# Attention with decay, then an expert layer: the first unit's second product taken by halves of the output columns, its weights loaded by the same halves, and a third score bank in the first four slots

## The chip, the core and the metric

The kernel runs on one core of a Trainium2 chip. Five engines work side by side on it, each through its own list of instructions in order: TensorE (PE in the profile; PEld is its loading of weights), VectorE (DVE), ScalarE (ACT), GpSimd (POOL) and SyncE (SP). They wait for each other through semaphores. DMA transfers are issued by POOL (through a software queue), SP and ACT. PSUM, where TensorE writes, has eight banks of 512 fp32 columns per partition.

The metric is the device time of one execution in microseconds, the median of several runs. Before the change it is 342.13 us (three runs, 341.74 to 342.63).

## The reference

Eight batches of eight heads, 576 positions, 64 elements a head. Scores get a decay that comes from cumulated logarithms of `f`, a causal mask and a softmax; the heads' outputs, side by side, are 4608 tokens of 512. The expert layer follows.

```python
scores = scale * np.matmul(q, k.transpose(0, 1, 3, 2))
log_f = np.log(np.clip(f, 0.0001, 1.0))
cum = np.cumsum(log_f, axis=-1)
scores = np.where(causal, -1e9, scores + (cum[:, :, :, None] - cum[:, :, None, :]))
attn = softmax(scores)
x = concat_heads(np.matmul(attn, v))          # 4608 x 512
h = x @ w_in                                  # 512 x 2048
out = (h - np.tanh(h)) @ w_out                # 2048 x 512
```

## The kernel before

The order of all instructions is written out by hand (`manual_schedule` over all five engines): what Python calls first stands first in its engine's list.

**Slots.** The work of attention goes by pairs of heads, 32 pairs (8 batches of 4). Pair p is computed in slot p, and `att_items(p)` lists what a slot holds: seven score tiles (ti = 0 to 6) of pair p, the transposes of q and k for pair p + 1, the second attention product of pair p - 1 (`values`), and the turning of that product into the ring `XR` that feeds the expert layer (`turn`). `LOADS` hangs DMA loads and some vector work on places (slot, ti).

- `scores` (L357 to L376): a tile of scores goes to a PSUM bank, ScalarE takes the exponential (L366) into a tile `e`, and from batch 1 on POOL cuts it causally (L376). In batch 0 (slots 0 to 3) a small matmul with `late` (L360) does the cut. The banks come from the pool `ps_sc` (two buffers); in batch 0 the small tile ti = 3 has the bank of `ps_tr`.
- `trans` (L303, copies L314 on ScalarE, L316 on VectorE): six transposes of q or k into one bank, then two copies (even and odd positions) into `QT` or `KT`. `copies` says which engine makes which copy: "VV" both VectorE.
- `values` (L394): 15 small matmuls a head; then `divide` on VectorE (L403 to L405) makes `xn`.
- `turn`: in batch 0 five transposes on TensorE (L422) and a copy on ScalarE (L423) into `XR`; later two transposing DMAs.
- `unread(n)` (L567): n matmuls of 128 columns whose result nobody reads. `start` issues 99 of them; in slot 0 `att_items` adds 4 at ti = 0, 5 and 6 each, and in slots 1 to 3 it adds 2 at ti = 0 and 2 at ti = 6.

**The expert layer** goes by units of 512 tokens. `mlp1` (L453) makes 16 tiles of the first product; ScalarE takes tanh (L458) and VectorE adds (L464) into `GQ`. For unit 0 `mlp2_plain` (L494) makes the second product: 16 steps of four matmuls with 512 columns; four steps fill a bank with 128 tokens by 512 output columns over all 16 tiles of `GQ`, four tiles a step, and ScalarE copies the bank out (L498). The later units use seven products of half size instead of eight (`mlp2`, L518), with sums of weights that `weights` makes once on VectorE (L283) at the places `SPOTS`. Steps of this layer are spread over the slots from slot 4 on (`TAKE`).

**Loads.** POOL issues nearly all loads in order into one software queue with eight semaphores, so the n-th load waits until the one eight before it has landed. `bulk` issues what is left of batch 0 (q, then k for heads 4 to 7, the decay rows chi, cq and clo, then v). The weights `w_in` come in two halves in slots 1 and 2, `w_out` in two halves of its rows in slot 4, and behind them q and k of batch 2.

Of the kernel before, what the change touches and what calls it, by code (L numbers as in the profile page):

```python
# [21 lines left out]
def kernel(  # L22
# [191 lines left out]

    def bulk():
        (k_hi, chi_0), (k_lo, clo_0), (q_hi, cq_0) = aug_rows(0)
        load_qk(qn, q, 0, 4, H)
        nc.gpsimd.dma_start(out=k_hi, in_=chi_0)
        load_qk(kn, k, 0, 4, H)
        nc.gpsimd.dma_start(out=q_hi, in_=cq_0)  # L220
        nc.gpsimd.dma_start(out=k_lo, in_=clo_0)
        for n in range(NJ - 1):
            load_v_block(0, n, 2, H)

# [1 line left out]
        nc.gpsimd.dma_start(out=win[:, :, f0:f1],  # L226
                            in_=moe_w_in[:, f0:f1].rearrange("(c p) f -> p c f", p=P))

    def load_wout(t0, t1):
        nc.gpsimd.dma_start(out=wout[:, t0:t1, :],  # L230
                            in_=moe_w_out[t0 * P:t1 * P, :].rearrange("(t p) e -> p t e", p=P))

    LOADS = {(0, 1): [lambda: load_qk(qn, q, 1, 0, 2), lambda: load_qk(kn, k, 1, 0, 2)],
             (0, 4): [lambda: load_qk(qn, q, 1, 2, 4), lambda: load_qk(kn, k, 1, 2, 4)],
# [2 lines left out]
             (1, 5): [lambda: load_qk(kn, k, 1, 4, H)],  # L237
             (2, 1): [lambda: load_v_rest(1), lambda: load_v_head(1, 0)],
             (2, 4): [lambda: load_v_head(1, 1), lambda: load_win(DFF // 2, DFF)],
             (4, 0): [lambda: load_wout(0, NFT // 2)],  # L240
             (4, 2): [lambda: load_wout(NFT // 2, NFT)]}
    for n in range(NJ - 1):
        LOADS.setdefault((3, n), []).append(lambda n=n: load_v_block(1, n, 2, H))
    def add(where, fn, *args):
        LOADS.setdefault(where, []).append(lambda: fn(*args))

    for b in range(2, B):
        p0 = (b - 1) * NPAIR
        at_q = [(p0 - 2, n + 2) for n in range(NJ)]
        at_k = [(p0, n) for n in range(NJ)]  # L250
        at_v = [(p0 + 1, n) for n in range(NJ)]
        to_q, to_k = (p0 - 1, 1), (p0 + 1, 4)
        on_q = p0
        on_k = (p0 + 3, 0), (p0 + 3, 2), (p0 + 4, 1), (p0 + 4, 4)
        if b == FAR:
            at_q = [(p0 - 1, n) for n in range(NJ)]
            to_q, on_q = (p0, 4), p0 + 3
            on_k = (p0 + 3, 2), (p0 + 3, 4), (p0 + 4, 0), (p0 + 4, 4)
        add((p0, 0), load_aug, b)
        for n in range(NJ):  # L260
            if n < NJ - 1:
                add(at_v[n], load_v_block, b, n, 0, H)
            else:
                add(at_v[n], load_v_rest, b)
            if b < FAR:
                continue
            add(at_q[n], load_block, qb, q, b, n)
            add(at_k[n], load_block, kb, k, b, n)
            add(to_q, turn_block, TQ[b % 2], qb, b, n)
            add(to_k, turn_block, TK, kb, b, n)  # L270
        if b < FAR:
            add((p0, 5), load_qk, qn, q, b, 0, H)
            add((p0, 6), load_qk, kn, k, b, 0, H)
            continue
        for n, (c, a) in enumerate(((0, 0), (0, 1), (2, 0), (2, 1))):
            add(on_k[n], place, KT, TK, b, a, c, 2, "V")
            add((on_q, (1 if b == FAR else 3) + n), place, QT, TQ[b % 2], b, a, c // 2, 1, "A")
            if c:
                add((on_q + 1, 1 + 2 * a), place, QT, TQ[b % 2], b, a, c, 2, "V")
# [2 lines left out]
        ks = slice(n * NK // 2, (n + 1) * NK // 2)  # L282
        nc.vector.tensor_tensor(out=o[:, ks, :], in0=x[:, ks, :], in1=y[:, ks, :], op=ALU.subtract)  # L283

    SPOTS = [(7, 1), (7, 3), (7, 5), (8, 1), (8, 3), (8, 5), (9, 5), (10, 5)]
    for i, (o, x, y) in enumerate(((W1, B12, B11), (W2, B22, W1), (W4, B21, W2), (B12, B22, B12))):
        for n in range(2):
            LOADS.setdefault(SPOTS[2 * i + n], []).append(lambda o=o, x=x, y=y, n=n: weights(o, x, y, n))
# [51 lines left out]
             4: (0, 1, 1, P), 5: (0, 1, 1, P), 6: (0, 2, 320, P)}  # L340

    def scores(b, c, ti):
        if b == 0 and ti == LAST:
            ps = ps_tr.tile([P, UW], FP32, tag="tr", name="ps")
        else:
            ps = ps_sc.tile([P, 512], FP32, tag="sc", name="ps")
# [62 lines left out]
        if not hold:  # L409
            release()  # L410

    def turn(b, c):
        xn = XN.pop((b, c))
        r0 = b % 4 * S
        if b == 0:
            x32 = m_bank("x32")
            if c == NPAIR - 1:
                M_AT[0] -= 1
            xt = x32.bitcast(FP16)[:, 0:S]
            for ib in (NJ - 1, 0, 1, 2, 3):  # L420
                w0 = min(ib * P, S - P)
                nc.tensor.transpose(out=xt[:, w0:w0 + P], in_=xn[:, ib, :], identity=id16)  # L422
            nc.scalar.activation(out=XR[:, c, r0:r0 + S], in_=xt, func=AF.Copy)  # L423
            return
        nc.sync.dma_start_transpose(out=XR[:, c, r0:r0 + S - D].rearrange("p (n t) -> p n t", t=P),
                                    in_=xn[:, 0:NJ - 1, :].rearrange("p n d -> p (n d)"))
        nc.sync.dma_start_transpose(out=XR[:, c, r0 + S - D:r0 + S], in_=xn[D:P, NJ - 1, :])
# [58 lines left out]
        nc.vector.tensor_tensor(out=LHS[name](u, i)[:, ks], in0=LHS[x](u, i)[:, ks], in1=LHS[y](u, i)[:, ks], op=op)  # L486

    def mlp2_plain(u, s):
        m, part = divmod(s, 4)
        if part == 0:  # L490
            M2[u] = bank("ops")
        ops = M2[u]
        for ft in range(part * 4, part * 4 + 4):
            nc.tensor.matmul(out=ops, lhsT=GQ[(u, ft % NK // 4)][:, ft // NK, ft % 4, m * P:(m + 1) * P],  # L494
                             rhs=wout[:, ft, :], start=(ft == 0), stop=(ft == NFT - 1))
        if part == 3:
            ost = tmp.tile([P, DM], FP32, tag="ost", name="ost", bufs=3)
            nc.scalar.activation(out=ost, in_=ops, func=AF.Copy)  # L498
            r0 = u * UW + m * P
            nc.sync.dma_start(out=out[r0:r0 + P, :], in_=ost)  # L500

    STEPS = [("A11", B11, "x"), ("S3", B12, "y"), ("A12", B21, "x"), ("S2", W2, "y"),
             ("S1", W1, "v"), ("A22", W4, "z"), ("S4", B22, "v")]
# [57 lines left out]
        else:  # L561
            give(0, 1, plus, M2["m7"])

    def unread(n):
        idle = ps_tr.tile([P, UW], FP32, tag="tr", name="idle")
        for i in range(n):
            nc.tensor.matmul(out=idle[:, i % 4 * P:i % 4 * P + P], lhsT=warm, rhs=warm, start=True, stop=True)  # L567

# [33 lines left out]
    def att_items(p):  # L602
        def put(fn, *args):
            items.append((lambda: fn(*args), True))
# [6 lines left out]
        for ti in range(len(TILES)):  # L611
            if here and (p > 0 or ti > 1):
                put(scores, *here, ti)
            if p == 1 and ti == 6:
                items.append((lambda: const_rows(1), False))
                items.append((lambda: load_aug(1), False))
            if early and ti in (0, 6) or p == 0 and ti == 5:
                put(unread, 2 if p else 4)
            if p == 1 and ti == 3:
                put(last)  # L620
            for load in LOADS.get((p, ti), ()):
# [10 lines left out]
                if ti in (4, 5):  # L632
                    put(mlp1, 0, ti - 4, 1)
            if ti == at_k and p < 2 * NPAIR - 1 and p != NPAIR:
                put(trans, *after, kn, KT, early, "VV")
            if p == NPAIR:
                if ti == 1:
                    put(turn, *pairs[p - 2])
                    put(values, *before)
                    put(mlp1, 0, 0, 0)  # L640
                elif ti == 2:
                    put(mlp1, 0, 1, 0)
                    put(turn, *before)
                    put(trans, *after, kn, KT, early, "VV")
            elif early and ti in (2, 3) and before:
                put(values, *before, (ti - 2,))
            elif not early and ti == 2 and before:
                put(values, *before, (0, 1), p == NPAIR + 2)
            if p < NPAIR:
                if ti == 1 and p > 1:  # L650
                    put(turn, *pairs[p - 2])
            elif p > NPAIR and ti == 3:
                items.append((release, False))
                put(turn, *before)
# [65 lines left out]
```

## Time and profile before

| | before |
|---|---|
| median of the runs | 342.13 us (341.74 to 342.63) |
| the profiled execution | 341.94 us |
| its span (first to last instruction) | 340.2 us |
| TensorE busy | 332.2 us (98%) |
| VectorE busy | 263.2 us (77%) |
| ScalarE busy | 235.0 us (69%) |
| POOL busy | 161.6 us (48%) |
| share of TensorE in the chain that ended last | 95% |
| first TensorE work of slots 1, 2, 3 and 4 | 14.74, 18.90, 23.53, 28.14 us |

The profile gives, for each engine, how long it was busy and, before an instruction, how long the engine sat idle and what ended that idle time. A row of the timeline reads: start in us, duration in us, engine, line, operation, output <- inputs with their shapes, how many are merged, and in brackets the idle time in front and its releaser. Matmuls are pipelined: a row's duration holds the latency of its last matmul, so the next row can start before it ends, and a bracket counts less than the hole between two rows of work.

### The profile page before, as it was taken

The page shows a single profiled execution, that of the slowest core. Times are in us where ns is not written, and L with a number is a line of the kernel's source. Part 1 is how long each engine was busy: PE and PEld are TensorE (multiplying, and loading weights), DVE is VectorE, ACT ScalarE, POOL GpSimd, SP SyncE. Part 2 cuts the span into 40 slices and gives each one's busy share as a digit, 9 for nine tenths or more (in the row PEclk, how much of TensorE's full clock was granted, in tenths as well). Part 3 has the DMA queues.
Part 4 walks back from the last instruction along what each step waited for, and adds up shares of the span by engine and source line. Part 5 has one row for each costly group of instructions (what it writes and reads, how often), then busy time and mean ns, then how long its engine had stood idle before and what let it go on. Part 6 is the DMA issues. An engine that isn't in the chain of part 4 may idle for free.

```text
span 340.2 us, 8658 instructions
## 1 busy us (share of the span) xinstructions
PE 332.2 (98%) x3271; PEld 231.8 (68%) x3271; DVE 263.2 (77%) x516; ACT 235.0 (69%) x440; POOL 161.6 (48%) x321
## 2 busy tenths in 40 slices
PE   8889999999999999999999999999999999999995
PEld 8676555555588458855788888656875686486485
DVE  8898888658887788678967886688668766966864
ACT  6887777888987886778677867787558742632630
POOL 8876746685657673776377547632322210000000
PEclk9999999999999999999999999999999999999999
DMA  9999999999999998999999998990131023002003
GB/s 121 146 181 200 190 200 168 170 145 161 135 100 177 157 116 90 130 186 120 115 114 168 129 125 99 178 124 13 51 113 14 19 59 102 0 33 92 3 14 109
DMA packets 144941, 38.86 MB, mean 114 GB/s; under 512 B 128188, under 2 KB 143276, under 8 KB 144900
## 3 DMA queue, kind: packets, MB, share of 16 engines
q0 software_dynamic: 92512, 18.39, 74.2%
q1 hardware_dynamic: 52356, 19.88, 30.7%
q8 instruction: 25, 0.41, 0.5%
q14 instruction: 16, 0.13, 0.1%
q10 hardware_dynamic: 32, 0.06, 0.1%
HBM read 36.90 MB, written 9.44 MB: 136 GB/s over the span
## 4 chain that ended last, share of the span: by engine, by line
PE 95%; ACT 3%; issue 1%; DVE 0%; ACTq 0%
PE hps L453 37%; PE ops L518 29%; PE ps L357 13%; PE av L394 9%; PE ops L494 3%; PE idle L567 2%; ACT e L366 2%; PE t L303 2%; PE ps L360 1%; PE x L422 0%; ACT W L575 0%; ACT KT L314 0%; ACT XR L423 0%; ACT W L314 0%; ACT th L458 0%
## 5 line engine op out<-in xcount | busy, mean ns | idle before, releaser
L453 PE MATMUL hps<-XR,win 128*128 128x512 f16 (+1 forms) x640 | 140.9, 357 | 0.3 <-ACT XR L423 0.2
L458 ACT ACTIVATE th<-hps 128x512 f32<-128x512 f32 x144 | 86.6, 602 | 55.1 <-PE hps L453 52.4
L366 ACT ACTIVATE e<-ps 128x512 f16<-128x512 f32 x192 | 110.5, 598 | 10.8 <-PE ps L357 6.9
L464 DVE TENSOR_TENSOR gq<-hps,th 128x512 f16<-128x512 f32 x144 | 98.2, 687 | 24.9 <-ACT th L458 23.4
L376 POOL TENSOR_SCALAR_AFFINE_SELECT e<-e 128x128 f16<-128x128 f16 x168 | 59.9, 358 | 71.9 <-ACT e L366 69.5
L453 PEld LDWEIGHTS <-win 128*128 128x128 f16 x640 | 57.7, 97 | 48.7 <-issue 0.7
L357 PE MATMUL ps<-QT,KT 67*128 67x512 f16 (+1 forms) x372 | 74.4, 276 | 2.2 <-ACT e L366 1.8
L518 PEld LDWEIGHTS <-gq 128*128 128x128 f16 x640 | 60.3, 97 | 11.1
L518 PE MATMUL ops<-wout,gq 128*128 128x256 f16 x512 | 63.2, 272 | 0.0
L357 PEld LDWEIGHTS <-KT 67*128 67x128 f16 x372 | 35.5, 98 | 24.3 <-issue 1.3
L394 PEld LDWEIGHTS <-e 128*128 128x128 f16 x896 | 32.3, 97 | 3.8
L394 PE MATMUL av<-vn,e 128*128 128x65 f16 x896 | 33.6, 193 | 0.0
L131 POOL DMA_DIRECT2D vn<-in_v_dram x32 | 27.9, 876 | 7.3 <-DMA win<-in_moe_w_in_dram 3.0
L518 PE MATMUL ops<-W,sq 128*128 128x256 f16 x256 | 31.2, 272 | 0.0
L405 DVE TENSOR_TENSOR xn<-av,rs 128x640 f16<-128x640 f32 x32 | 26.4, 825 | 1.1
L518 PEld LDWEIGHTS <-sq 128*128 128x128 f16 x256 | 24.2, 98 | 3.4
L376 POOL TENSOR_SCALAR_AFFINE_SELECT el<-el 128x128 f16<-128x128 f16 x28 | 9.2, 330 | 27.8 <-ACT el L366 27.3
L108 POOL DMA_DIRECT2D kn<-in_k_dram x25 | 21.1, 845 | 1.5 <-issue 1.3
L108 POOL DMA_DIRECT2D qn<-in_q_dram x25 | 21.1, 845 | 1.4 <-issue 0.9
L403 DVE TENSOR_SCALAR rs<-av 128x10 f32<-128x10 f32 x32 | 5.2, 163 | 19.0 <-PE av L394 17.8
L533 ACT ACTIVATE m<-ops 128x512 f32<-128x512 f32 x16 | 9.5, 596 | 10.9 <-PE ops L518 10.9
L486 DVE TENSOR_TENSOR gq<-gq 128x512 f16<-128x512 f16 x32 | 16.6, 519 | 0.0
(92 smaller groups left out, 317.6 us busy)
## 6 DMA issues: line engine op xcount, KB each, us to landing
out_dram<-ost SPq DMA_DIRECT2D x34, 256.0 KB
vn<-in_v_dram POOLq DMA_DIRECT2D x24, 128.0 KB, 5.6
qn<-in_q_dram POOLq DMA_DIRECT2D x20, 128.0 KB, 5.0
kn<-in_k_dram POOLq DMA_DIRECT2D x20, 128.0 KB, 4.7
win<-in_moe_w_in_dram POOLq DMA_DIRECT2D x2, 1024.0 KB, 12.2
wout<-in_moe_w_out_dram POOLq DMA_DIRECT2D x2, 1024.0 KB, 14.9
XR<-xn SPq DMA_TRANSPOSE x56
vn<-in_v_dram POOLq DMA_DIRECT2D x12, 64.0 KB, 5.3
```

Source lines behind the costliest of these rows:

```text
L108: nc.gpsimd.dma_start(out=dst[b % 2][0:pn, n, :].rearrange("p (h d) -> p h d", h=H), in_=src[b, :, n * P:n * P + pn, :].rearrange("h p d - ...
L131: nc.gpsimd.dma_start(out=vn[b % 2][:, n, h0:h1, 0:D], in_=v[b, h0:h1, n * P:(n + 1) * P, :].rearrange("h p d -> p h d"))
L357: nc.tensor.matmul(out=ps[:, col:col + n], lhsT=kt[0:rows, h, j * P:(j + 1) * P], rhs=qt[0:rows, h, i0:i0 + n], start=True, stop=cut == 0)
L366: nc.scalar.activation(out=e[:, lo:hi], in_=ps[:, lo:hi], func=AF.Exp, scale=qscale)
L376: nc.gpsimd.affine_select(out=view, in_=view, compare_op=ALU.is_ge, fill=0.0, base=0, pattern=pat, channel_multiplier=-1)
L394: nc.tensor.matmul(out=av[:, a, ib, :], lhsT=E.pop((b, c, a, j, ib)), rhs=vn[b % 2][:, j, 2 * c + a, 0:D + 1], start=(j == 0), stop=(j == ib))
L405: nc.vector.tensor_tensor(out=xn.rearrange("p i (a d) -> p a i d", a=2), in0=av[:, :, :, 0:D], in1=rs.to_broadcast([P, 2, NJ, D]), op=ALU. ...
L453: nc.tensor.matmul(out=hps[:, o:o + n], lhsT=win[:, ci, ft * P:(ft + 1) * P], rhs=XR[:, ci, t:t + n], start=(ci == 0), stop=(ci == NCH - 1))
L458: nc.scalar.activation(out=th, in_=hps, func=AF.Tanh, scale=-1.0)
L464: nc.vector.tensor_tensor(out=GQ[(u, i)][:, half, kt, :], in0=hps, in1=th, op=ALU.add)
L486: nc.vector.tensor_tensor(out=LHS[name](u, i)[:, ks], in0=LHS[x](u, i)[:, ks], in1=LHS[y](u, i)[:, ks], op=op)
L518: nc.tensor.matmul(out=ps[:, m, :], lhsT=LHS[lhs](u, kt // 4)[:, kt % 4, m * P:(m + 1) * P], rhs=rhs[:, kt, :], start=(fresh and (apart or ...
```

## The change

- **Second product of unit 0.** A step of `mlp2_plain` now makes eight matmuls with 256 columns: for one half of the output columns (e), one pair of token blocks (mp), one block of it (m) and one half of the 16 tiles of `GQ`. Four steps still fill one bank, now two blocks of 128 tokens by 256 columns. The first step reads tiles 0 to 7, the second tiles 8 to 15.
- **Loads of w_out** go by the same halves of the columns: the first at (4, 0), the second at (5, 1). q and k of batch 2 move up to (4, 2) and (4, 5), so they are issued between the two. v of batch 2 moves from slot 5 to slot 6, q of batch 3 by one tile within slot 7.
- **The sums of weights** (`SPOTS`) move from slots 7 to 10 into slots 8 to 10.
- **Loads of batch 0** (`bulk`): q and k of heads 4 and 5, then the decay rows, then q and k of heads 6 and 7.
- **Slots 0 to 3.** In slots 1 to 3 every third score tile goes to the bank of `ps_tr`, so three banks take turns; in slot 0 nothing changes there. `values` of the second head comes after ti = 4 instead of ti = 3. In slots 2 and 3 the copy into `XR` is on VectorE instead of ScalarE, and the first of the two copies of k on ScalarE instead of VectorE.
- **Unread matmuls**: slot 0 gets 2, 14, 4 and 6 at ti = 0, 2, 5 and 6; slot 1 gets 8 at ti = 6 in a bank of `ps_m`; slots 2 and 3 get none.

```diff
     def bulk():
-        load_qk(qn, q, 0, 4, H)
+        load_qk(qn, q, 0, 4, 6)
+        load_qk(kn, k, 0, 4, 6)
         nc.gpsimd.dma_start(out=k_hi, in_=chi_0)
-        load_qk(kn, k, 0, 4, H)
         nc.gpsimd.dma_start(out=q_hi, in_=cq_0)
         nc.gpsimd.dma_start(out=k_lo, in_=clo_0)
+        load_qk(qn, q, 0, 6, H)
+        load_qk(kn, k, 0, 6, H)
...
-    def load_wout(t0, t1):
-        nc.gpsimd.dma_start(out=wout[:, t0:t1, :],
-                            in_=moe_w_out[t0 * P:t1 * P, :].rearrange("(t p) e -> p t e", p=P))
+    def load_wout(e0, e1):
+        nc.gpsimd.dma_start(out=wout[:, :, e0:e1], in_=moe_w_out[:, e0:e1].rearrange("(t p) e -> p t e", p=P))
...
-             (4, 0): [lambda: load_wout(0, NFT // 2)],
-             (4, 2): [lambda: load_wout(NFT // 2, NFT)]}
+             (4, 0): [lambda: load_wout(0, HE)],
+             (5, 1): [lambda: load_wout(HE, DM)]}
...
-        at_v = [(p0 + 1, n) for n in range(NJ)]
+        at_v = [(p0 + (1 if b >= FAR else 2), n) for n in range(NJ)]
...
         if b == FAR:
-            at_q = [(p0 - 1, n) for n in range(NJ)]
+            at_q = [(p0 - 1, n + 1) for n in range(NJ)]
...
         if b < FAR:
-            add((p0, 5), load_qk, qn, q, b, 0, H)
-            add((p0, 6), load_qk, kn, k, b, 0, H)
+            add((p0, 2), load_qk, qn, q, b, 0, H)
+            add((p0, 5), load_qk, kn, k, b, 0, H)
...
-    SPOTS = [(7, 1), (7, 3), (7, 5), (8, 1), (8, 3), (8, 5), (9, 5), (10, 5)]
+    SPOTS = [(8, 1), (8, 3), (8, 5), (9, 1), (9, 3), (9, 5), (10, 3), (10, 5)]
...
     def scores(b, c, ti):
-        if b == 0 and ti == LAST:
+        if b == 0 and (((c - 1) * len(TILES) + ti) % 3 == 0 if c else ti == LAST):
             ps = ps_tr.tile([P, UW], FP32, tag="tr", name="ps")
...
-    def turn(b, c):
+    def turn(b, c, vector=False):
...
-            nc.scalar.activation(out=XR[:, c, r0:r0 + S], in_=xt, func=AF.Copy)
+            if vector:
+                nc.vector.tensor_copy(out=XR[:, c, r0:r0 + S], in_=xt)
+            else:
+                nc.scalar.activation(out=XR[:, c, r0:r0 + S], in_=xt, func=AF.Copy)
...
     def mlp2_plain(u, s):
-        m, part = divmod(s, 4)
-        if part == 0:
-            M2[u] = bank("ops")
-        ops = M2[u]
-        for ft in range(part * 4, part * 4 + 4):
-            nc.tensor.matmul(out=ops, lhsT=GQ[(u, ft % NK // 4)][:, ft // NK, ft % 4, m * P:(m + 1) * P],
-                             rhs=wout[:, ft, :], start=(ft == 0), stop=(ft == NFT - 1))
-        if part == 3:
+        e, mp, m, half = s // 8, s // 4 % 2, s // 2 % 2, s % 2
+        if s % 4 == 0:
+            M2[u] = bank("ops").rearrange("p (m e) -> p m e", m=2)
+        ops, t0 = M2[u], (2 * mp + m) * P
+        for ft in range(half * NK, half * NK + NK):
+            nc.tensor.matmul(out=ops[:, m, :], lhsT=GQ[(u, ft % NK // 4)][:, half, ft % 4, t0:t0 + P],
+                             rhs=wout[:, ft, e * HE:(e + 1) * HE], start=(m == 0 and ft == 0),
+                             stop=(m == 1 and ft == NFT - 1), skip_group_check=True)
+        if s % 4 == 3:
...
-    def unread(n):
-        idle = ps_tr.tile([P, UW], FP32, tag="tr", name="idle")
+    def unread(n, lent=False):
+        idle = m_bank("idle") if lent else ps_tr.tile([P, UW], FP32, tag="tr", name="idle")
...
-            if early and ti in (0, 6) or p == 0 and ti == 5:
-                put(unread, 2 if p else 4)
+            if p == 0 and ti in (0, 2, 5, 6):
+                put(unread, {0: 2, 2: 14, 5: 4, 6: 6}[ti])
+            if p == 1 and ti == 6:
+                put(unread, 8, True)
...
-                put(trans, *after, kn, KT, early, "VV")
+                put(trans, *after, kn, KT, early, "AV" if early and p > 1 else "VV")
...
-            elif early and ti in (2, 3) and before:
-                put(values, *before, (ti - 2,))
+            elif early and ti in (2, 4) and before:
+                put(values, *before, (ti // 2 - 1,))
...
-                    put(turn, *pairs[p - 2])
+                    put(turn, *pairs[p - 2], True)
```

## The prediction

> **What bounds the kernel now.** I read the page first, then busy time by stretches, the chain that ended last, the timelines of TensorE, VectorE and ScalarE over slots 0 to 8, and the issues and landings of the loads.
>
> ```profile
> span 340.2 us, 8658 instructions
> PE 332.2 (98%) x3271; PEld 231.8 (68%) x3271; DVE 263.2 (77%) x516; ACT 235.0 (69%) x440; POOL 161.6 (48%) x321
> 10.00:20.00 10.00, 8.14 (x129) 6.46 (x127) 8.54 (x14) 8.56 (x17) 9.82 (x16) 1.00 1.46 157
> 20.00:30.00 10.00, 8.95 (x169) 7.52 (x167) 9.71 (x17) 8.35 (x18) 5.47 (x8) 1.00 1.33 190
> 70.00:80.00 10.00, 10.00 (x85) 5.37 (x83) 5.37 (x10) 8.26 (x15) 6.61 (x13) 1.00 1.85 148
> ```
>
> The three lower rows are stretches (span; busy time of PE, PEld, DVE, ACT, POOL; granted clock). From 70 us on TensorE has no hole, so whatever the change does must show as the time at which TensorE gets to 70 us, plus what its own matmuls cost. Between 20 and 30 us it is VectorE that is nearly full (9.71 of 10). What it does there:
>
> ```profile
> 12.74 1.62 DVE L316 COPY KT<-t 64x576 f16<-64x576 f16 x2
> 15.58 1.62 DVE L316 COPY QT<-t 64x576 f16<-64x576 f16 x2 [1.23 <-PE t L303]
> 17.22 1.61 DVE L316 COPY KT<-t 64x576 f16<-64x576 f16 x2
> 18.86 0.17 DVE L403 TENSOR_SCALAR rs<-av 128x10 f32<-128x10 f32 x1
> 20.06 1.62 DVE L316 COPY QT<-t 64x576 f16<-64x576 f16 x2
> ...
> 29.00 1.62 DVE L316 COPY QT<-t 64x576 f16<-64x576 f16 x2
> ```
>
> Four copies and one division (18.86 to 20.06, 1.20) take 4.48 us, and from 20.06 to 29.00 the same comes twice more, 4.47 each, without a hole. So VectorE sets the pace of slots 1 to 3, and only its hole of 1.23 before 15.58, or less work on it, can shorten them. TensorE and ScalarE wait for each other too:
>
> ```profile
> 12.08 0.19 PE L357 MATMUL ps<-W,W 88*128 88x64 f16 x1 [0.74 <-ACT W L314]
> 14.74 0.38 PE L357 MATMUL ps<-QT,KT 67*128 67x512 f16 x1 [0.51 <-ACT e L366]
> 23.04 0.30 PE L357 MATMUL ps<-QT,KT 67*128 67x320 f16 x1 [0.46 <-ACT e L366]
> 22.39 1.08 ACT L366 ACTIVATE e<-ps 128x512 f16<-128x512 f32 x2 [0.39 <-PE ps L360]
> 25.31 0.65 ACT L423 ACTIVATE XR<-x 128x576 f16<-128x576 f16 x1
> 25.84 0.60 ACT L366 ACTIVATE e<-ps 128x512 f16<-128x512 f32 x1
> 26.32 0.30 ACT L366 ACTIVATE el<-ps 128x128 f16<-128x128 f32 x1
> ```
>
> With two banks TensorE waits for the exponential and ScalarE then for TensorE (0.46 and 0.39 in slot 2). Where nothing is waited for, an exponential starts 0.48 after the one before (25.84 to 26.32).
>
> **The change, part by part.** *Start of slot 1.* Its first scores need the copies of k, done at 12.74 + 1.62 = 14.36, and the decay row clo:
>
> ```profile
> L221 POOL DMA_DIRECT2D KT<-clo x1: 521/521/521, 10.1 to 10.1; - x1
> DMA to landing us min/median/max: 4.5/4.5/4.5
> ```
>
> That row lands at 14.6, just before the scores' 14.74. In the change two of the four heads' loads are issued behind the decay rows, so the rows land sooner; I take the copies of k to be last, and with 0.07 for the hand-over the scores at 14.43 (-0.31). Two unread matmuls between these scores and the transposes go (-0.11). VectorE starts on q at 15.16 instead of 15.58: -0.42.
>
> *VectorE in slots 2 and 3.* Each loses a copy of k (0.80) and gets the copy into XR. No row shows that copy on VectorE. The nearest:
>
> ```profile
> L423 ACT ACTIVATE XR<-x 128x576 f16<-128x576 f16 x4 | 2.6, 647 | 0.3 <-PE x L422 0.3
> L486 DVE TENSOR_TENSOR sq<-gq 128x512 f16<-128x512 f16 x32 | 11.5, 420 | 0.0
> L316 DVE COPY KT<-t 64x576 f16<-64x576 f16 x18 | 14.4, 799 | 2.1 <-PE t L303 1.9
> L314 ACT ACTIVATE KT<-t 64x576 f16<-64x576 f16 x4 | 3.3, 814 | 0.1
> ```
>
> It lies between 0.42 (16-bit numbers side by side, both ways) and 0.80 (from PSUM, scattered by the copy). The XR copy reads and writes side by side, so I take 0.45: 0.35 less for VectorE in each slot, 0.70 in two; the ends are 0.76 and 0. The Trainium skill, in "VectorE: DVE Perf Modes", section "Why PSUM operands drop a tier", says that a PSUM operand still allows two 16-bit elements a cycle. No run here shows it yet; by the cycle table of that page the copy would be an estimated 0.43 at the double rate and 0.73 at the single one, and the sum below -0.30 or +0.30.
>
> ScalarE gives up 0.65 and gets 0.81 per slot; with three banks it needs 6 x 0.48 + 0.30 + 0.81 = 4.0, VectorE 1.62 + 0.80 + 0.45 + 1.20 = 4.07. So ScalarE just fits below, the third bank is what lets it fit, and VectorE stays the bound. The copy of k on ScalarE must end before VectorE's half, which waits for it; VectorE does 1.62 of q first, ScalarE one exponential: hidden by about 0.4. `values` of head 1 moves behind one more tile, some 0.3 of TensorE, while the division that reads it stands behind 3.2 of copies on VectorE: hidden. Early gain: -0.42 - 0.70 = -1.12 at slot 4, ends -0.42 and -1.18.
>
> *Unread matmuls.* 14 x 56 ns = 0.78 lie in the hole in front of 12.08 (0.74, and the latency of the small matmul before it, which the bracket leaves out); 6 before slot 1 and 8 at the end of slot 1 lie before the copies of k are done. Nothing, or 0.1 if that cover goes.
>
> *The second product's steps.* The second step now reads tiles 8 to 15 instead of 4 to 7:
>
> ```profile
> 53.81 1.03 PE L494 MATMUL ops<-wout,gq 128*128 128x512 f16 x4
> 54.67 0.42 PE L303 MATMUL t<-id,qn 96*128 96x96 f16 x6
> 47.67 0.69 DVE L464 TENSOR_TENSOR gq<-hps,th 128x512 f16<-128x512 f32 x1 [0.78 <-ACT th L458]
> 53.98 1.28 DVE L464 TENSOR_TENSOR gq<-hps,th 128x512 f16<-128x512 f32 x2
> 56.02 0.38 PE L357 MATMUL ps<-QT,KT 67*128 67x320 f16 x2
> ...
> 56.41 0.28 PEld L303 LDWEIGHTS <-kn 96*128 96x128 f16 x6 [0.29 <-DMA kn<-in_k_dram]
> ```
>
> Tiles 14 and 15 are the last two sums, 53.98 to 55.26, and from 47.67 on VectorE is busy with work whose inputs are there, so its end moves with everything else and not faster. The step that ended at 54.67 can load its last weights only at 55.3 and ends at about 55.53: +0.86 (at least 55.26 - 54.67 = +0.59, if the last load and matmul cost nothing). Behind it on TensorE stand the transposes of q and all that follows, and no hole takes it back. This is a new wait.
>
> *Loads.* k of batch 2 landed at 56.4 and TensorE waited 0.17 (from the end of the scores, 56.24). It now stands in front of half of w_out, 1 MB, and lands earlier by that much: -0.17, and the early gain does not run into that landing. The second half of w_out lands where k landed, or up to 1.4 later, and is first read by the ninth step. POOL issues two loads more (0.7 each) ahead of the first half of w_in:
>
> ```profile
> 63.84 1.03 PE L494 MATMUL ops<-wout,gq 128*128 128x512 f16 x4
> 26.86 0.82 POOL L131 DMA_DIRECT2D vn<-in_v_dram  x1 [3.03 <-DMA win<-in_moe_w_in_dram]
> 30.34 0.92 PE L453 MATMUL hps<-XR,win 128*128 128x512 f16 x3
> 75.34 0.17 DVE L403 TENSOR_SCALAR rs<-av 128x10 f32<-128x10 f32 x1 [3.36 <-PE av L394]
> win<-in_moe_w_in_dram POOLq DMA_DIRECT2D x2, 1024.0 KB, 12.2
> 79.70 0.69 DVE L464 TENSOR_TENSOR gq<-hps,th 128x512 f16<-128x512 f32 x1 [0.39 <-ACT th L458]
> ```
>
> The ninth step stands at 63.84, 6 us behind. w_in landed before 26.86, now by 28.3; its first reader moves from 30.34 to 29.2. Hidden, with 0.9 to spare. POOL's masks of slot 4 stand behind these loads, but the second attention product that reads them runs a slot later. v of batch 2 and q of batch 3 have most of a slot to spare: nothing. SP keeps its order; unit 0's four stores have lines half as long, and nobody waits for them.
>
> *Sums of weights.* Six of eight move later. One falls in the hole of 3.36 before 75.34, one before the add at 79.70, which waits for tanh anyway (0.39), one a slot later between adds that wait in the same way. Nothing; at most 0.3 of the hole is missing.
>
> *Half as wide.* 64 matmuls of 512 columns become 128 of 256. In the chain:
>
> ```profile
> 298.52 12.23 PE ops L518 x112
> 310.75 13.81 PE hps L453 x64
> 1.13 5.13 PE idle L567 x47
> 7.10 2.12 PE idle L567 x38
> ```
>
> 128 x 12.23/112 - 64 x 13.81/64 = 13.98 - 13.81 = +0.17.
>
> *Sum.* -1.12 + 0.86 - 0.17 + 0.17 = -0.26 on the profiled execution's 341.94, so 341.68. That execution lies 0.19 below the runs' median of 342.13; in terms of the median, 341.87, say 341.9. With the ends of the copy (0.42, 0.80) and of the wait (0.59, 0.86) the sum runs from -0.59 to +0.44: 341.5 to 342.6.
>
> **Rivals.** *Faster, the new wait does not come.* If VectorE reaches tiles 14 and 15 by the time TensorE wants them, -1.12 - 0.17 + 0.17 = -1.12: 341.0. For it: VectorE did wait 0.78 for tanh at 47.67, so it is not always behind. Against it: nine ops whose inputs are there stand between there and 53.98.
>
> *The third bank buys nothing.* VectorE set the pace all along; if the XR copy costs it 0.80, only -0.42 is left: +0.44, 342.6. For it: 9.71 of 10 busy; the copy reads PSUM like those of 0.80. Against it: the side-by-side row of 0.42.
>
> *Slower: w_in lands late.* One mechanism, in slot 4: two more issues on POOL before it, and TensorE wants it at 29.2. By the row above the two halves of w_in took 12.2 us to land in the median. With the first half issued 1.4 later, at an estimated 17.8, and 12.2 behind it, it lands at 30.0, 0.8 late; every us past 29.2 is one on the end. With 14 it is 2.6 late: 344.5. From 1.3 late on it decides.
>
> *Slower: a cold array.* The first 47 unread matmuls took 5.13 us, 109 ns each, the 38 later ones 56 ns: the array ran at half speed at first, while the granted clock read 1.00. The change takes 8 unread matmuls out of slots 2 and 3 and leaves TensorE holes of up to 0.7. If one such stretch came back it would cost 5.13 - 2.63 = 2.5: 344.4. Against it: the hole before 12.08 did not bring it back. The Trainium skill ("TensorE: Matmul & The Clock Gate", section "What's actually happening") puts the return to half speed behind an idle window of about 3.4 us; by that rule it stays away here, and the trace agrees so far.
>
> **How the numbers follow.** Likeliest (-0.26): 0.36. Third bank without effect: 0.20. Both lie within 0.3% (1.03 us, about what a measurement of this kernel can tell from no change): same 0.56. No new wait, or an early gain beyond my end: 0.27, just past 0.3%. Late w_in 0.09, cold array 0.04, a place that I did not see 0.04: slower 0.17. The range reaches to the faster rival, 340.8, and to 342.9, past the second; it leaves out the two slower rivals. The likeliest case alone has 341.5 to 342.6.
>
> **What would show it.** Right: QT copies of slot 4 at about 27.9 instead of 29.00; XR copies on VectorE near 0.45; no idle time on TensorE before scores from ScalarE's exponentials in slots 1 to 3; an idle time of 0.6 to 0.9 before a weight load of the second step, ended by VectorE's add; no wait for k of batch 2. Wrong: XR copies of 0.75 or more; a wait for w_in at 29; matmuls at twice their duration in slots 2 to 4; holes between 76 and 95 us, where the sums of weights went.

## The result and the profile after

The changed kernel takes 341.41 us (median of 14 runs, 341.06 to 342.18) beside 342.17 for the kernel before on the same chip: 0.76 us less, ratio 0.9976 with a 95% interval of 0.9968 to 0.9984. That is within the 0.3% which the prediction calls no change, though the interval leaves out 1. The profiled execution took 341.6 us (before: 341.94). Some executions of these kernels, eight of twelve in e6 and three of twelve in e7 below, ran at a granted clock of 0.985 to 0.995 instead of 1.00, which by itself is 1.7 to 5.1 us of 340, and took some 2 to 5 us longer; what brings them on is open.

The head of the page of the changed kernel, and its stretches (span; busy time of PE, PEld, DVE, ACT, POOL; granted clock):

```profile
span 339.9 us, 8804 instructions
PE 333.0 (98%) x3345; PEld 237.7 (70%) x3345; DVE 262.5 (77%) x516; ACT 235.1 (69%) x440; POOL 163.7 (48%) x323
10.00:20.00 10.00, 9.50 (x153) 7.63 (x150) 8.96 (x15) 9.09 (x18) 9.82 (x15) 1.00 1.25 126
20.00:30.00 10.00, 9.52 (x172) 7.55 (x171) 9.66 (x19) 8.81 (x18) 5.92 (x10) 1.00 1.21 193
70.00:80.00 10.00, 9.73 (x94) 6.34 (x93) 6.05 (x12) 7.82 (x15) 7.14 (x14) 1.00 2.33 158
```

TensorE is fuller from 10 to 30 us (9.50 and 9.52 instead of 8.14 and 8.95); up to 20 us a part of that is unread matmuls, of which slot 0 now has 26 instead of 12 and slot 1 has 8 instead of 4. Between 70 and 80 us, where it had no hole before, 0.27 are missing. VectorE is still nearly full from 20 to 30, so it still sets the pace there, at a shorter slot. Its timeline over slots 2 and 3:

```profile
21.21 0.79 DVE L317 COPY KT<-t 64x576 f16<-64x576 f16 x1
22.04 0.46 DVE L425 COPY XR<-x 128x576 f16<-128x576 f16 x1
22.41 0.16 DVE L404 TENSOR_SCALAR rs<-av 128x10 f32<-128x10 f32 x1
22.60 0.22 DVE L405 RECIPROCAL rs<-rs 128x10 f32<-128x10 f32 x1
22.85 0.82 DVE L406 TENSOR_TENSOR xn<-av,rs 128x640 f16<-128x640 f32 x1
23.59 1.61 DVE L317 COPY QT<-t 64x576 f16<-64x576 f16 x2
25.16 0.82 DVE L317 COPY KT<-t 64x576 f16<-64x576 f16 x1
26.01 0.46 DVE L425 COPY XR<-x 128x576 f16<-128x576 f16 x1
...
27.57 0.79 DVE L317 COPY QT<-t 64x576 f16<-64x576 f16 x1
```

From one pair of q copies to the next pass 3.98 us in slot 3 (23.59 to 27.57; 4.47 before) and 3.89 in slot 2 (19.70 to 23.59). The copy into XR takes 0.46, and the next instruction starts 0.37 behind its start. The copies of slot 4 start at 27.57 instead of 29.00: 1.43 earlier.

Then the second product on TensorE, and the loading of its weights:

```profile
50.75 1.04 PE L498 MATMUL ops<-wout,gq 128*128 128x256 f16 x8
52.36 1.19 PE L498 MATMUL ops<-wout,gq 128*128 128x256 f16 x7
53.86 0.28 PE L498 MATMUL ops<-wout,gq 128*128 128x256 f16 x1 [0.32 <-DVE gq L468]
53.98 0.42 PE L304 MATMUL t<-id,qn 96*128 96x96 f16 x6
55.55 0.42 PE L304 MATMUL t<-id,kn 96*128 96x96 f16 x6
...
53.26 0.10 PEld L498 LDWEIGHTS <-gq 128*128 128x128 f16 x1 [0.36 <-DVE gq L468]
53.86 0.10 PEld L498 LDWEIGHTS <-gq 128*128 128x128 f16 x1 [0.50 <-DVE gq L468]
```

The second step starts 1.45 early (52.36; before 53.81), the transposes of q behind it only 0.69 early (53.98; 54.67): the new wait takes 0.76. VectorE's last sums end 1.45 early too (53.81; before 55.26), so they came no faster than the rest. The last time VectorE was idle ahead of them is the same in both kernels, 0.78 for ScalarE's tanh, here at 46.22 (before at 47.67), and the last sums start 6.31 behind that row in both:

```profile
46.22 0.69 DVE L468 TENSOR_TENSOR gq<-hps,th 128x512 f16<-128x512 f32 x1 [0.78 <-ACT th L462]
52.53 1.28 DVE L468 TENSOR_TENSOR gq<-hps,th 128x512 f16<-128x512 f32 x2
```

The wait for k of batch 2 is gone: from the transposes of q to those of k pass 1.57 (1.74 before), so -0.17. And a wait that the prediction did not have:

```profile
74.36 0.81 PE L457 MATMUL hps<-XR,win 128*128 128x512 f16 x3
75.45 0.38 PE L457 MATMUL hps<-XR,win 128*128 128x512 f16 x1 [0.27 <-DMA XR<-xn]
...
67.83 1.24 SPq L429 DMA_TRANSPOSE XR<-xn  x1
69.12 1.27 SPq L431 DMA_TRANSPOSE XR<-xn  x1
```

Three matmuls of 0.22 from start to start would put the fourth at 75.01; it starts at 75.45, 0.44 late, because a transposing DMA issued at 67.83 or 69.12 had not landed. From there on the two traces run side by side. In the chain of waits of both, the last common stretch begins with these rows, of the kernel before and of the changed one:

```profile
277.72 6.99 PE ops L518 x64
```

```profile
277.39 6.99 PE ops L523 x64
```

**A ledger.** The start of the program varies: the first scores of slot 0 come at 9.04 to 9.56 us in the profiles of this case (9.06 before, 9.10 here). I count from there, so that kernels can be compared by one profile each, to three marks: first scores of slot 1, first step of the second product, and the row of 64 matmuls above. The first scores and the first step of the kernel before are these rows:

```profile
9.06 0.38 PE L357 MATMUL ps<-W,W 88*128 88x512 f16 x1
52.20 1.03 PE L494 MATMUL ops<-wout,gq 128*128 128x512 f16 x4
```

| kernel | first scores | to slot 1 | to the first step | to the 64 matmuls | against before |
|---|---|---|---|---|---|
| before | 9.06 | 5.68 | 43.14 | 268.66 | |
| changed | 9.10 | 5.37 | 41.65 | 268.29 | -0.37 |
| changed, second profile (e9) | 9.21 | 5.37 | 41.66 | 267.83 | -0.83 |

So up to the second product the change gains 1.49. Of this the new wait costs 0.76, the wait for k gives 0.17, and some 0.1 is left for the narrower matmuls: -1.49 + 0.76 - 0.17 + 0.1 = -0.8, which is what the second profile shows (-0.83). The 0.1 is what remains of such sums (0.06 in e9, 0.10 in e1, 0.12 in e7), not a row of its own. The first profile shows 0.46 less, of which the late DMA is 0.44.

### The profile page after: what moved, and what is told of

Same layout as the page of the kernel before. It is cut to its first block, busy times and chain, and to the rows that moved or that the text cites. A ratio compares the mean times of both kernels' runs of the same rounds, so it can differ in the third digit from the quotient of the medians.

```text
span 339.9 us, 8804 instructions
## 1 busy us (share of the span) xinstructions
PE 333.0 (98%) x3345; PEld 237.7 (70%) x3345; DVE 262.5 (77%) x516; ACT 235.1 (69%) x440; POOL 163.7 (48%) x323
## 4 chain that ended last, share of the span: by engine, by line
PE 85%; DVE 8%; DMA 2%; ACT 2%; issue 1%; ACTq 0%
PE hps L457 35%; PE ops L523 29%; PE ps L358 11%; PE av L395 7%; DMA XR<-xn 2%; PE ops L498 2%; DVE KT L317 2%; DVE QT L317 1%; ACT e L367 1%; DVE gq L468 1%; PE t L304 1%; DVE xn L406 1%; DVE W L317 1%; PE x L423 0%; DVE TQ L195 0%
## 5 line engine op out<-in xcount | busy, mean ns | idle before, releaser
L523 PE MATMUL ops<-wout,gq 128*128 128x256 f16 x512 | 63.2, 272 | 0.0
L498 PE MATMUL ops<-wout,gq 128*128 128x256 f16 x128 | 16.9, 272 | 0.4 <-DVE gq L468 0.3
L317 DVE COPY QT<-t 64x576 f16<-64x576 f16 x18 | 14.4, 801 | 3.5 <-PE t L304 3.4
```

The costliest lines, as they stand in the source:

```text
L317: nc.vector.tensor_copy(out=to, in_=of)
L523: nc.tensor.matmul(out=ps[:, m, :], lhsT=LHS[lhs](u, kt // 4)[:, kt % 4, m * P:(m + 1) * P], rhs=rhs[:, kt, :], start=(fresh and (apart or ...
```

## The experiments

Each was timed beside the kernel before, three or four kernels to a chip; ratios are to that kernel's runs there (medians 342.25, 342.36 and 342.36). My theory was that VectorE's copies pace slots 1 to 3, and that the second step's tiles take half of the gain back; the rivals were that the third score bank made the gain, and that the step's wait comes only because TensorE runs early.

**e4: the copies go back.** Copies into XR on ScalarE and both copies of k on VectorE, the rest as changed.

```diff
-                put(trans, *after, kn, KT, early, "AV" if early and p > 1 else "VV")
+                put(trans, *after, kn, KT, early, "VV")
-                    put(turn, *pairs[p - 2], True)
+                    put(turn, *pairs[p - 2])
```

> The changed kernel with the copies into XR on ScalarE and both copies of k on VectorE again in slots 2 and 3 (third score bank and everything else as changed). Theory, VectorE's copies set the pace of these slots: its work per slot is 4.47 instead of 3.98, slot 4 starts 2 x 0.49 = 0.98 later, and of that the hole of 0.45 at 75 us is taken back: 341.41 + 0.53 = 341.9. Rival, the third score bank alone made the early gain: slot 4 starts no later than 0.2, the time stays at 341.4.

342.23 us, ratio 1.0003 (0.9994 to 1.0011): nothing is left of the gain. VectorE's timeline of this kernel:

```profile
19.66 1.61 DVE L317 COPY QT<-t 64x576 f16<-64x576 f16 x2
21.28 1.61 DVE L317 COPY KT<-t 64x576 f16<-64x576 f16 x2
22.93 0.17 DVE L404 TENSOR_SCALAR rs<-av 128x10 f32<-128x10 f32 x1
...
24.12 1.61 DVE L317 COPY QT<-t 64x576 f16<-64x576 f16 x2
```

The slot is 4.46 again (19.66 to 24.12), and the first step comes 42.75 after the first scores instead of 41.65: the swap of copies is worth 1.10. What is left of the early gain is 0.39: 0.29 before the first scores of slot 1 (14.43 - 9.04 = 5.39 against 5.68), and the rest between them and the q copies (0.74 against 0.84). The rival falls: with three banks, but without the swap, slots 2 and 3 are no shorter than before. The end is 268.93, so +0.27 against before, as the sum -0.39 + 0.76 - 0.17 + 0.1 = +0.3 has it; I had expected 0.3 less, for I took the late DMA's 0.45 as won back, and that did not belong to the median. By the medians alone the swap is worth less, 0.74 (342.23 here and 341.41 for the changed kernel, each beside the kernel before on its chip, 342.25 and 342.17); that kernel's 29 single times on this chip run from 341.50 to 344.61, so I go by the trace for differences of a few tenths.

**e5: two banks.** The third bank goes, the swap stays.

```diff
-        if b == 0 and (((c - 1) * len(TILES) + ti) % 3 == 0 if c else ti == LAST):
+        if b == 0 and ti == LAST:
```

> The changed kernel with two score banks in slots 1 to 3, as before (the third only for the small tile). Theory, ScalarE only just fits beside VectorE's shorter slot and the third bank is what lets it fit: waits between TensorE and ScalarE of 0.4 to 0.5 us come back in each slot and take at least 0.3 per slot, so about 0.8 of the gain goes: 342.2. Rival, VectorE alone sets the pace and the third bank is idle help: within 0.2 of 341.4.

341.50 us, ratio 0.9969 (0.9954 to 0.9984). The first step comes 41.96 after the first scores, 0.31 later than with three banks. Its timeline has waits for ScalarE in front of the scores of slots 3 and 4; the third row is of the changed kernel, at the same place as the second:

```profile
22.93 0.38 PE L358 MATMUL ps<-QT,KT 67*128 67x512 f16 x1 [0.23 <-ACT e L367]
27.12 0.38 PE L358 MATMUL ps<-QT,KT 67*128 67x512 f16 x1 [0.18 <-ACT e L367]
```

```profile
26.86 0.38 PE L358 MATMUL ps<-QT,KT 67*128 67x512 f16 x1 [0.41 <-ACT e L367]
```

So only the first of these waits comes back, at half the size that I had put on it; in front of slot 4, where both kernels have two banks again, the changed kernel waits longer. What is lost shows on VectorE: from the q copies of slot 2 to those of slot 4 pass 8.15 (19.67 to 27.82) and 7.87 with three banks. The bank is worth 0.3 of the swap's 1.1, and next to nothing without the swap (e4). My "about 0.8 of the gain goes" was wrong; the rival (within 0.2) holds for the time, and misses the 0.31 of the trace only by a little.

**e6: the early part alone.** Slots 0 to 3 and the loads of batch 0 as changed; second product, its loads and all later ones as before.

```diff
-        load_qk(qn, q, 0, 4, H)
+        load_qk(qn, q, 0, 4, 6)
+        load_qk(kn, k, 0, 4, 6)
...
-        if b == 0 and ti == LAST:
+        if b == 0 and (((c - 1) * len(TILES) + ti) % 3 == 0 if c else ti == LAST):
...
-                    put(turn, *pairs[p - 2])
+                    put(turn, *pairs[p - 2], True)
```

> The kernel before with only the changes to the loads of batch 0 and to slots 0 to 3 (third bank, copies into XR on VectorE, one copy of k on ScalarE, unread matmuls, second attention product by heads); the second product and all later loads as before. TensorE reaches slot 8 about 1.5 us earlier. Theory, the landing of k of batch 2 is fixed by what stands ahead of it in POOL's queue, and 1 MB more stands ahead of it than in the changed kernel: the wait of 0.17 becomes 1.7 or more and eats the gain, 342.2 to 343.4. Rival, the loads move with the work because POOL issues them in step with it: 342.17 - 1.5 = 340.7 or a few tenths more.

345.75 us, ratio 1.0062 (1.0028 to 1.0096): slower than before. The single times stand in two groups, four from 342.13 to 342.97 and eight from 345.54 to 347.71; the profile is of the fastest one. TensorE's timeline there:

```profile
53.76 0.43 PE L305 MATMUL t<-id,qn 96*128 96x96 f16 x6 [0.29 <-DMA qn<-in_q_dram]
...
56.57 0.43 PE L305 MATMUL t<-id,kn 96*128 96x96 f16 x6 [1.08 <-DMA kn<-in_k_dram]
```

The early gain is there (first step 41.65 after the first scores), and both loads of batch 2 eat it: k is transposed at 56.57, no earlier than before (56.41), although TensorE is there 1.5 earlier. The load of k was issued at 37.2 and landed 19.3 later (before 36.9 and 19.4; in the changed kernel, where it stands ahead of half of w_out, 36.4 and 17.2). The end is 268.72, +0.06. So the theory holds for the trace: this landing does not move with TensorE's work, and moving q and k between the halves of w_out is what lets the early gain through. The four shorter times have the median 342.53, within the 342.2 to 343.4 that I expected; the median of all twelve is not, and the eight longer ones I had not foreseen.

**e7: the second product alone.** Its halves, its loads and the later sums of weights; slots 0 to 3 and the loads of batch 0 as before.

```diff
-             (4, 0): [lambda: load_wout(0, NFT // 2)],
-             (4, 2): [lambda: load_wout(NFT // 2, NFT)]}
+             (4, 0): [lambda: load_wout(0, HE)],
+             (5, 1): [lambda: load_wout(HE, DM)]}
...
-        m, part = divmod(s, 4)
+        e, mp, m, half = s // 8, s // 4 % 2, s // 2 % 2, s % 2
```

> The kernel before with only the second product by halves of the columns, the loads that go with it, and the sums of weights at their later places; slots 0 to 3 as before. Theory, the new wait for tiles 14 and 15 comes whatever the early slots do: +0.76, k of batch 2 no longer waited for -0.17, narrower matmuls +0.08: 342.17 + 0.67 = 342.8. Rival, the wait is there only because the early gain lets TensorE run into VectorE: 342.17 - 0.17 + 0.08 = 342.1.

342.64 us, ratio 1.0021 (0.9992 to 1.0049). Three of its twelve executions took 344.91 to 346.74; by the time alone this would be open, but the trace is plain:

```profile
53.84 1.19 PE L493 MATMUL ops<-wout,gq 128*128 128x256 f16 x7
55.34 0.28 PE L493 MATMUL ops<-wout,gq 128*128 128x256 f16 x1 [0.32 <-DVE gq L463]
55.46 0.42 PE L302 MATMUL t<-id,qn 96*128 96x96 f16 x6
```

The same hole with the same 0.32 before the last matmul, with TensorE 1.5 us later. VectorE's last idle time before these sums is again one for tanh (0.77, before the add at 47.70), and they start 6.30 behind that add, at 54.00. So they are late because VectorE's chain starts from work of TensorE and ScalarE that moves along, not because TensorE runs ahead. The 64 matmuls come at 269.33 after the first scores, +0.67 against before, the sum that was expected.

**e1: the other order of steps.** The second step takes tiles 0 to 7 of the other block; tiles 8 to 15 come in steps three and four.

```diff
-        e, mp, m, half = s // 8, s // 4 % 2, s // 2 % 2, s % 2
+        e, mp, half, m = s // 8, s // 4 % 2, s // 2 % 2, s % 2
```

> The changed kernel, except that the second product's second step takes the other block of tokens over tiles 0 to 7 and not tiles 8 to 15; those come in the third and fourth step. Theory: the 0.5 us that TensorE waits near 53 us for VectorE's last sums go, because the third step stands a good 2 us further on, and the transposes of q behind it come 0.76 earlier. How much of that reaches the end hangs on the hole of 0.45 at 75 us before the transposing DMA into XR has landed: if the landing moves with the work, 341.41 - 0.76 = 340.65; if it is fixed by the loads ahead of it in the queues, TensorE only waits longer there and the time stays at 341.4. Rival: VectorE is late for every step of the second product, so the third step waits in place of the second: 341.4, with an idle time ended by VectorE's add before the third step.

341.04 us, ratio 0.9962 (0.9947 to 0.9977). The two steps and the transposes now stand without a hole:

```profile
51.10 1.04 PE L498 MATMUL ops<-wout,gq 128*128 128x256 f16 x8
...
52.70 1.04 PE L498 MATMUL ops<-wout,gq 128*128 128x256 f16 x8
53.57 0.42 PE L304 MATMUL t<-id,qn 96*128 96x96 f16 x6
```

2.47 from the first step to the transposes of q, as before the change, and 3.23 with it (50.75 to 53.98): the 0.76. The third step finds its tiles, so the rival falls. The 64 matmuls come 267.07 after the first scores, 0.76 less than in e9. The median moved by less (about 0.4 beside the changed kernel's), and its single times spread from 340.45 to 341.97.

**e2 and e3: fewer loads beside the late DMA.** The five loads of k of batch 3 go two score tiles later, in e2 alone and in e3 together with e1's order.

```diff
-        at_k = [(p0, n) for n in range(NJ)]
+        at_k = [(p0, n + (2 if b == FAR else 0)) for n in range(NJ)]
```

> The changed kernel, with the five loads of k of batch 3 two score tiles later, so that fewer of them are in flight while the transposing DMAs into XR (issued at 67.8 and 69.1 us) run. Theory: those DMAs land late (about 75.4 us) because loads that moved behind the second half of w_out share the DMA engines with them; with fewer loads beside them they land in time, the hole of 0.45 goes, and the time is 341.41 - 0.45 = 340.96. Rival: the transposing DMAs are late for a reason of their own, or the hole is a matter of the one profiled execution: 341.4, hole still there.

> Both edits at once: the second step on tiles 0 to 7 of the other block, and the loads of k of batch 3 two score tiles later. Theory of two separate waits: 341.41 - 0.76 - 0.45 = 340.2, with neither idle time in the profile. Rival, the landing of XR is fixed by earlier loads: no better than the better of the two single edits, with a hole of up to 1.2 us at 75 us.

e2: 341.17 us, ratio 0.9973 (0.9964 to 0.9981), which can't be told from the changed kernel's 0.9976. e3: 340.51 us (five runs), ratio 0.9954 (0.9942 to 0.9967), where the sum of two separate waits was 340.2. Neither profile has the hole at 75 us, but that of e1 has none either, so these two don't show that the loads of k were the cause.

**e9, e10, e11: the hole at 75 us again.** The changed kernel once more, the kernel before with the later k of batch 3, and e3's kernel once more, on one chip.

> The changed kernel as it is, a second time, for the hole of 0.45 at 75 us. Theory, a transposing DMA into XR lands late in some executions only: this profile is likely to show no such hole, the end comes 0.86 before that of the kernel before (counted from the first scores), and single times spread over 0.5 or more above the lowest. Rival, the hole belongs to the change: it is there again, of 0.3 to 0.6.

> The kernel before with the loads of k of batch 3 two score tiles later. TensorE comes to the same place some 0.8 to 1.6 us later than in the changed kernels, so by the theory of a late transposing DMA there is less to gain: 342.17, within 0.2. Rival, crowded queues cost the kernel before as much: 341.8 or less.

> The other order of the second product's steps and the later loads of k of batch 3 together, once more beside the changed kernel on one chip. Theory of separate waits: 0.7 to 0.9 us under the changed kernel. Rival, the first result came from few runs of a quiet chip: 0.4 or less.

e9: 341.38 us, ratio 0.9962 (0.9937 to 0.9987). Its timeline at the place of the hole:

```profile
74.48 1.03 PE L457 MATMUL hps<-XR,win 128*128 128x512 f16 x4
75.34 0.23 PE L358 MATMUL ps<-QT,KT 67*128 67x64 f16 x2
```

All four matmuls in one row, no wait: the change does not bring the hole in every execution. Whether it brings it more often, two profiles can't show. e10: 342.61 us, ratio 1.0002 (0.9985 to 1.0019), no gain there. Its profile shows what else can come late in the kernel before:

```profile
15.76 0.38 PE L357 MATMUL ps<-QT,KT 67*128 67x512 f16 x1 [1.03 <-DMA KT<-clo]
```

The decay row clo, which the prediction had landing at 14.6, just before the scores at 14.74, held them until 15.76 in this execution. In the changed kernel it lands at 12.7 (issued at 10.1, 2.6 to landing):

```profile
L221 POOL DMA_DIRECT2D KT<-clo x1: 508/508/508, 10.1 to 10.1; - x1
DMA to landing us min/median/max: 2.6/2.6/2.6
```

e11: 340.54 us (12 runs, 340.37 to 341.20), ratio 0.9935 (0.9909 to 0.9961), 0.84 under the changed kernel on that chip. So the other order of the steps with the later k of batch 3 beats both kernels, by 1.8 us against the kernel before. Its mark is 276.34 - 9.05 = 267.29, 0.2 more than in e3, and most of that is lost at the matmul of the hole at 75 us. The row of four lasts 1.19 here and 1.11 in e8 below, which has the later loads of k too, instead of 1.03:

```profile
73.58 1.19 PE L457 MATMUL hps<-XR,win 128*128 128x512 f16 x4
```

```profile
73.57 1.11 PE L457 MATMUL hps<-XR,win 128*128 128x512 f16 x4
```

In both it is the fourth matmul that starts late (74.39 and 74.31, 0.38 and 0.31 behind the third instead of 0.22). The profile names no releaser there; that it is the same landing is argued from the place; if so, it stands close to TensorE's need with the later k too. How much the later k adds to the other order is open: the marks of e1 and e3 are both 267.07, while the medians are 341.04 and 340.51.

**e8: fewer unread matmuls at the start.** e3 with 30 instead of 38 of them before the first scores.

```diff
-        unread(38)
+        unread(30)
```

> The changed kernel with the other order of the second product's steps, k of batch 3 two score tiles later, and 30 instead of 38 unread matmuls before the first scores. In the six profiled executions so far these unread matmuls ended between 9.0 and 9.5 us, and VectorE's copy that the first scores need was there at 9.0. Theory: TensorE's own unread matmuls make the first scores late by 0.2 on average; 8 fewer are 0.45: 340.5 - 0.2 = 340.3. Rival: the array slows down in the hole, or the start is set by VectorE: 340.5 or more.

340.95 us, ratio 0.9969 (0.9941 to 0.9996), no better than e3. Its single times spread from 340.29 to 344.35; the profile is of one of the shorter ones (340.51). The first scores came at 9.04, when VectorE had them ready, and the 64 matmuls at 276.30 exactly as in e3, whose scores began 0.19 later: small holes along the way had taken it back, 0.09 of them between 73 and 82 us, nearly all at the fourth matmul above. What ends the others isn't settled.

## Why the prediction was right, and where it was off

The forecast was 341.9 with no change as the likeliest case; 341.41 lies within the likeliest case's class and within the range, a little under its own 341.5 to 342.6. The gain is three times the forecast one, 0.76 instead of 0.26, and 341.41 stands as near to the rival without the new wait (341.0) as to the forecast. "No change" held because it reaches to 1.03 either way; that the likeliest case and not that rival came true, the traces show and not the time. Point by point:

- **Start of slot 1, -0.42.** Right. To slot 1 it is 5.37 instead of 5.68 (-0.31, the number predicted), and VectorE's q copies follow after 0.75 instead of 0.84. The row of 14.74 puts its wait down to ScalarE's exponential, not to clo; but e5, with two banks and its exponentials at the same times (the last ends at 12.87 + 1.78 = 14.65 in both), has these scores at 14.45, so it was the row. That clo stops being a tie was read, but not that it can lose it by 1.03 (e10).
- **VectorE in slots 2 and 3, -0.70.** The right mechanism, and the term that was mis-sized most: it is 1.10 (e4). The copy into XR takes 0.46, as estimated (0.45). But I subtracted durations where starts count. The next instruction starts 0.37 behind the start of that copy, and with one copy of k gone the other one starts about 0.1 before the last q copy ends (21.21 is 1.51 behind 19.70, where the kernel before needed 1.63, 20.06 to 21.69). The rows of the changed kernel and of the one before:

```profile
19.70 1.61 DVE L317 COPY QT<-t 64x576 f16<-64x576 f16 x2
```

```profile
21.69 1.61 DVE L316 COPY KT<-t 64x576 f16<-64x576 f16 x2
```

  The Trainium skill, "VectorE: DVE Perf Modes", section "Two Vector instructions with no wait between them", gives a model for this: a Vector instruction has to wait for the end of all earlier ones if, among other cases, its input begins in another group of 32 partitions than the input read before from that memory. The copy that stayed on VectorE reads the upper 64 partitions of its bank like the q copy in front of it, and the instruction behind the XR copy reads from partition 0 like that copy; the trace agrees in both places (0.1 and 0.09 early). It agrees too where the partitions change: before, the k copy starts at 21.69, when the q copies have ended (20.06 + 1.62). No run here changes the partitions to test it.
- **The third bank lets ScalarE fit.** Right in kind. Without it 0.31 goes over all these slots (e5), where I had read 0.4 to 0.5 a slot from the old waits.
- **The new wait, +0.86.** Right in place and cause (the second step's weights wait for VectorE's add), 0.76 in size, within the ends 0.59 to 0.86. The transposes follow 0.17 behind the end of the last sums (52.53 + 1.28 = 53.81 to 53.98), where I had 0.27. e7 shows it without the early gain, e1 shows it gone.
- **k of batch 2, -0.17.** Right; and e6 shows what the sentence "the early gain does not run into that landing" was worth: all of it.
- **Half as wide, +0.17.** About 0.1, as a remainder: e1's sum leaves -1.59 + 1.52 + 0.17 = 0.10, with its first step 41.62 after the first scores (-1.52).
- **"v of batch 2 and q of batch 3 have most of a slot to spare: nothing."** True for themselves. Late in the first profile was a transfer that I had not listed, the transposing DMA of slot 7, by 0.44 in that one execution. What delayed it isn't settled.
- **Rivals.** The wait did come. The XR copy was not 0.80. w_in did not come late: its first half, issued at 17.68, landed 10.6 later, at about 28.3, and TensorE's first matmul with it started at 28.91 without a wait, with 0.6 to spare where I had 0.9. No stretch of matmuls at double duration came back in the profile of the changed kernel, and its 14 runs all read a granted clock of 0.999 or more.

With the terms as measured the sum is -0.39 - 1.10 + 0.76 - 0.17 + 0.10 = -0.80 on the execution's 341.94; the medians say -0.76. That these agree so closely is partly luck: the sum leaves out where each execution starts and which transfers come late in it, and the medians hold both.

## What to carry to other kernels

Work given back early by a faster stage is worth something only if the next fixed landing moves too: the same early gain of 1.5 us was worth nothing in the trace while k of batch 2 stood behind 2 MB of weights (e6). When work is split anew, look at which half of its inputs is finished last; here swapping two index bits kept those inputs for a step later and won back 0.76 that the split had cost (e1). And count an engine's instructions from start to start, in their new order, not by their durations.

## What the runs showed of the hardware that I had not expected

- The 47 unread matmuls at the start took 4.47 us in one execution (e4) and 5.19 in another (e1). In e4 TensorE then waited 0.47 for VectorE before the first scores at 9.04; in e1 they came at 9.48, with no wait before them. The 47 alone don't set it: in e3 they took 5.19 too, and the first scores came at 9.23. A common mark in the trace takes this out when profiles are compared.

```profile
1.13 4.47 PE L572 MATMUL idle<-warm 128*128 128x128 f16 x47 [1.13 <-DVE warm L141]
```

```profile
1.13 5.19 PE L572 MATMUL idle<-warm 128*128 128x128 f16 x47 [1.13 <-DVE warm L141]
```

- A copy of 128 x 576 from PSUM of 16-bit numbers side by side takes 0.46 us on VectorE (0.65 on ScalarE), beside 0.80 for 64 x 576 scattered. The Trainium skill, "VectorE: DVE Perf Modes", section "Why PSUM operands drop a tier", allows such a copy two elements a cycle. The trace agrees: the prediction's estimate at that rate was 0.43, at one element a cycle 0.73.
- One small transfer of 9 KB, issued at 10.1 or 10.2, landed after 2.6 us when it stood behind two loads of 144 KB (the changed kernel), and after 4.5 (before) and 5.4 (e10) where it stood behind two of 288 KB, which the change splits.
